# Batch 1's query and key loads in six-row pieces with 128x128 transposes, and the last output rows in two column halves

## The chip, the cores and the metric

The kernel runs on one core of a Trainium2 chip. The metric is the device time of one execution in microseconds. The kernel before took 255.05 us, the median of six runs (254.12 to 255.78).

## The reference

Attention over 4 batches of 8 heads, 768 positions and 64 dimensions per head, with a mask that keeps the first 4 positions (the sinks) and a window of 128; then a gated feed-forward layer over the 3072 tokens (512 wide, 1536 hidden).

```python
scores = scale * np.matmul(q, k.transpose(0, 1, 3, 2))
keep = is_sink | in_window
scores = np.where(keep, scores, -1000000000.0)
a = np.exp(scores - np.max(scores, axis=-1, keepdims=True))
attn_out = np.matmul(a / (np.sum(a, axis=-1, keepdims=True) + 1e-09), v)
x = attn_out.transpose(0, 2, 1, 3).reshape(B * S, H * D)
gate = np.maximum(x @ w_gate, 0.0)
out = gate * (x @ w_val) @ w_out
```

## The kernel before

Two heads make a unit; unit i belongs to batch i // 4. A unit's queries and keys are needed with the dimension on the partitions (64 of each head), in bf16. They get there in three ways:

- Batch 0, in halves (`load_half`, `cast_half`, `T_half`), with transposes on TensorE.
- Batch 1 (units 4 to 7): `load_kq` (L111) loads with (head, position group of 12) on the partitions, so that each partition holds 12 consecutive rows of one head; `cast_kq` (L145) makes bf16 on GpSimd; `T` (L275) turns the tile on TensorE in 64x64 pieces (L282), 12 for each of the two heads and each of key and query. ScalarE copies the turned keys out of PSUM (L286), VectorE the queries (L287), and VectorE then lays out the odd key tiles (L199) and the sinks (L195) beside the keys.
- Batches 2 and 3 (units 8 to 15): `load_rows` (L173) loads six rows of both heads to a partition, `cast_rows` (L178) casts on GpSimd, `to_dram` (L183) writes the result to DRAM (query first, then key), and `turn` (L188) reads it back by a DMA with transpose. GpSimd lays out the odd tiles and the sinks.

Scores are made in segments (`Sg`, L314): matmuls into a pair of PSUM banks (L324), exponential on ScalarE (L328), mask on VectorE (L335). The two pairs of banks alternate for all callers of `pair()`, so a segment waits until the pair's last reader is done; the queries turned by `T` lie in such a pair too, the keys in bank G[3]. `W` (L382) multiplies the exponentials by the values, and VectorE divides by the sum (L393, L394).

The order of work is written out by hand: 96 slots, each with one chunk of the feed-forward layer (`chunk`, L410: gate matmuls L417, Relu on ScalarE L420, value matmuls L422, product on VectorE L424). A table `plan` gives the attention steps that follow a chunk, and a table `prep` the loads and casts ahead of it. `T` of units 4 to 7 follows the chunks of slots 11, 12, 15 and 16; their scores run in slots 13 to 20. Unit 8's scores begin in slot 25 and unit 9's in slot 27. Each engine works through its instructions in this order, and so do the queues that issue DMAs: SP issues nearly all of them, GpSimd those of the weights.

The second layer (`ffn2`, L431) multiplies 128 tokens' hidden values by the output weights in 12 matmuls of 512 columns (L437); ScalarE copies the bank to SBUF (L441) and SP stores it (L442). These matmuls fill in behind the chunks; the last six tiles of 128 tokens follow, partly or wholly, the last chunk, with three banks in turn.

Of the kernel before, what the change touches and what calls it, by code (L numbers as in the profile page):

```python
# [9 lines left out]
F32 = mybir.dt.float32  # L10
BF16 = mybir.dt.bfloat16
# [8 lines left out]
def kernel(  # L20
# [12 lines left out]
    nc = tc.nc  # L33
    B, H, S, D = q.shape
# [3 lines left out]
    d_model, d_ff = moe_w_gate.shape  # L38
    KO = d_model // 128
    FM = d_ff // 128  # L40

    NR, PR = 12, 64

    const = ctx.enter_context(tc.tile_pool(name="const", bufs=1))
    gspool = ctx.enter_context(tc.tile_pool(name="gsp", bufs=3))
    outpool = ctx.enter_context(tc.tile_pool(name="outp", bufs=3))
# [3 lines left out]
    NQ, NE, NT = 3, 4, 4  # L50
    kf = [const.tile([128, S], F32, name=f"kf{i}") for i in range(NQ)]
    qf = [const.tile([128, S], F32, name=f"qf{i}") for i in range(NQ)]
# [4 lines left out]
    qT = [x[:, 0:S] for x in KQ]  # L57
# [4 lines left out]
    qn = [const.tile([128, S], BF16, name=f"qn{i}") for i in range(2)]  # L62
    kn = [const.tile([128, S], BF16, name=f"kn{i}") for i in range(2)]
    wg = const.tile([128, KO, d_ff], BF16, name="wg")
    wv = const.tile([128, KO, d_ff], BF16, name="wv")
    wo = const.tile([128, FM, d_model], BF16, name="wo")
    xT = [const.tile([128, NP, S], BF16, name=f"xT{i}") for i in range(2)]
    hT = [const.tile([128, FM, S], BF16, name=f"hT{i}") for i in range(2)]
    ident = const.tile([128, 128], BF16, name="ident")
# [38 lines left out]

    U = [Unit(i) for i in range(B * NP)]

    def load_kq(u):  # L111
        for x, dst in ((k, kf[u.i % NQ]), (q, qf[u.i % NQ])):
            nc.sync.dma_start(out=dst[:], in_=x[u.b, 2 * u.p:2 * u.p + 2].rearrange("h (p n) d -> (h p) (n d)", n=NR))


    HALF = S // 2
    half = lambda bufs, c: bufs[c // 2 % len(bufs)][:, c % 2 * HALF:c % 2 * HALF + HALF]
# [24 lines left out]
    def cast_v(b, j, rows=128, copy=nc.gpsimd.tensor_copy):  # L142
        copy(vn[b % 2][0:rows, j, :, 0:64], vf[0:rows, j, :, :])  # L143

    def cast_kq(u):  # L145
        for src, dst in ((kf[u.i % NQ], kn[u.i % 2]), (qf[u.i % NQ], qn[u.i % 2])):
            nc.gpsimd.tensor_copy(dst[:], src[:])

    def gate(u):

        nc.scalar.copy(kf[u.i % NQ][0:1, 0:2], warm[0:1, :])
# [2 lines left out]
    ND = 2 * NP  # L154
# [14 lines left out]
        for x in range(2):  # L169
            ready[u.b, u.p, x] = True  # L170


    def load_rows(u):  # L173
        for x, dst in ((q, qf), (k, kf)):
            nc.sync.dma_start(out=dst[u.i % NQ][:].rearrange("p (h e) -> p h e", h=2),
                              in_=x[u.b, 2 * u.p:2 * u.p + 2].rearrange("h (p n) d -> p h (n d)", n=6))

    def cast_rows(u):  # L178
        for src, dst in ((qf, qn), (kf, kn)):
            nc.gpsimd.tensor_copy(dst[u.i % 2][:].rearrange("p (n h d) -> p h n d", n=6, h=2),  # L180
                                  src[u.i % NQ][:].rearrange("p (h n d) -> p h n d", n=6, h=2))

    def to_dram(u):  # L183
        for i, x in enumerate((qn, kn)):
            nc.sync.dma_start(out=kqd[u.i - ND][i * S:i * S + S, :].rearrange("(p n) c -> p (n c)", n=6),
                              in_=x[u.i % 2][:])

    def turn(u):  # L188
# [86 lines left out]
    def T(u):  # L275
        t = u.i % NT
        tk, tq = G[3][:], pair()[:, 0, :]
        for x, ps in ((kn[u.i % 2], tk), (qn[u.i % 2], tq)):
            for n in range(NR):
                for h in range(2):  # L280
                    r = slice(64 * h, 64 * h + 64)
                    nc.tensor.transpose(ps.bitcast(BF16)[r, 64 * n:64 * n + 64], x[r, 64 * n:64 * n + 64], ident[r, r])  # L282
        vk, vq = (ps.bitcast(BF16)[:, 0:S].rearrange("d (n p) -> d p n", p=PR) for ps in (tk, tq))
        e = kE[t]
        to = lambda ap: ap.rearrange("d (p n) -> d p n", n=NR)
        nc.scalar.copy(to(e[:, 0:S]), vk)  # L286
        nc.vector.tensor_copy(to(qT[t]), vq)  # L287
        odd_tiles(u, nc.vector.tensor_copy)

    def T_half(c):  # L290
# [140 lines left out]
    def ffn2(b, t, m):  # L431
        if m == 0:
            ops = OP[tail[0]]
            opn[0] += 1
            opend[b, t] = ops[opn[0] % len(ops)]
        op = opend[b, t]
        nc.tensor.matmul(out=op, lhsT=hT[b % 2][:, m, t * 128:(t + 1) * 128], rhs=wo[:, m, :],  # L437
                         start=m == 0, stop=m == FM - 1)
        if m == FM - 1:
            ot = outpool.tile([128, d_model], F32, name="ot")  # L440
            nc.scalar.copy(ot[:], op)  # L441
            nc.sync.dma_start(out=out[b * S + t * 128:b * S + (t + 1) * 128, :], in_=ot[:])  # L442

    with tc.manual_schedule():
# [112 lines left out]
        for s, (b, g, m) in enumerate(slots):  # L557
            for x in prep[s]:
                if x[0] == "kq":
                    cast_kq(U[x[1]])  # L560
                elif x[0] == "load":
                    if x[1] < 7:
                        gate(U[x[1]])
                    load_kq(U[x[1]])
                elif x[0] == "half":
                    cast_half(x[1])
                elif x[0] == "w":
                    load_w(*x[1:])
                elif x[0] == "wo":
                    for c in range(3):  # L570
                        load_wo(c)
                elif x[0] == "rows":
                    load_rows(U[x[1]])
                elif x[0] == "castrows":
                    cast_rows(U[x[1]])
                elif x[0] == "td":
                    to_dram(U[x[1]])
                elif x[0] == "setup3":
                    setup3()
                elif x[0] == "setup2":  # L580
                    setup2(x[1])
                elif x[0] == "xd":
                    x_to_dram(U[x[1]])
                elif x[0] == "xturn":
                    x_turn(U[x[1]])
                elif x[0] == "turn":
                    turn(U[x[1]])
                elif x[0] == "sinks":
                    odd_tiles(U[x[1]], nc.gpsimd.tensor_copy)
                elif x[0] == "lv":  # L590
                    for j in x[2:] or range(7):
                        load_v(x[1], j)
                else:
                    cast_v(*x[1:])
            chunk(b, g, m)
            if s == 23:
                f2 += [lambda t=t, mm=mm: ffn2(0, t, mm) for t in range(6) for mm in range(FM)]
            for what, i, x in plan[s]:
                if what == "F":
                    for _ in range(i):  # L600
                        f2.popleft()()
                elif what == "X":
                    X(U[i])
                elif what == "T":
                    T(U[i])
                elif what == "H":
                    T_half(NP + i)
                elif what == "S":
                    Sg(U[i], x)
                elif what == "W":  # L610
                    W(U[i])
                else:
                    V(U[i], x)
            for _ in range(3 if s > 23 else 0):
                if f2:
                    f2.popleft()()
            if b > 0 and m == FM - 1:
                f2 += [lambda b=b, t=t, mm=mm: ffn2(b, t, mm) for t in range(3 * g, 3 * g + 3) for mm in range(FM)]
# [38 lines left out]
```

The softmax here doesn't subtract the row's maximum and nothing guards it: scores larger than these inputs give would overflow.

## Time and profile before

| what | value |
|---|---|
| the profiled execution | 254.73 us, its span 253.0 us |
| TensorE busy | 239.3 us (95% of the span) |
| VectorE busy | 131.0 us |
| ScalarE busy | 117.3 us |
| GpSimd busy | 68.1 us |
| query copies of units 4 to 7 on VectorE (L287) | 4 of 0.944 us |
| key copies of units 4 to 7 on ScalarE (L286) | 4 of 0.80 us |
| granted TensorE clock, mean | 0.997 |
| moved by DMA | 40.09 MB, mean 158 GB/s |

Time in the profile is counted from the start of the span. A line of the timeline gives start, length, engine, line of the kernel, operation, tiles and shapes, and how many instructions were merged; in brackets stands the engine's idle time just ahead of it and what ended it. The chain that ended last is followed back from the last instruction: at each step to what released it, or to the instruction before it on its engine. PE is TensorE, DVE VectorE, ACT ScalarE, POOL GpSimd, SP the engine that issues DMAs.

### The profile page before, as it was taken

How to read it: one execution, taken by the hardware profiler on the slowest of the kernel's cores; microseconds unless marked ns; L12 is line 12 of the kernel's file. 1: busy time of each engine (PE TensorE's matmuls, PEld its weight loads, DVE VectorE, ACT ScalarE, POOL GpSimd, SP SyncE). 2: the span in 40 equal slices, each digit the busy share in tenths (PEclk: the TensorE clock that was granted, in tenths of full speed). 3: DMA queues.
4: the chain of work that ended last, by engine and by line, in shares of the span. 5: the costliest groups of instructions: out<-in, count | busy, mean ns of one | idle time of the engine just before them, and what ended most of it. 6: DMA issues, size and time to landing. Idle time of an engine off the chain costs nothing.

```text
span 253.0 us, 5586 instructions
## 1 busy us (share of the span) xinstructions
PE 239.3 (95%) x2197; PEld 140.4 (55%) x2219; DVE 131.0 (52%) x249; ACT 117.3 (46%) x215; POOL 68.1 (27%) x118
## 2 busy tenths in 40 slices
PE   7779999898999799999999999999999999999993
PEld 2445566566675456666555556666555555555441
DVE  7586889999892556654225465744223222322000
ACT  3656942585854654542345674532333332333111
POOL 6694494777024227403003700000000000000000
PEclk9999999999999999999999999999999999999998
DMA  7999999999999999979899711433211101111132
GB/s 188 276 258 192 192 179 340 279 237 259 268 248 234 191 225 318 299 212 213 169 189 240 142 41 33 114 98 75 79 44 43 41 0 44 43 41 44 48 118 83
DMA packets 75571, 40.09 MB, mean 158 GB/s; under 512 B 53529, under 2 KB 71449, under 8 KB 75545
## 3 DMA queue, kind: packets, MB, share of 16 engines
q1 hardware_dynamic: 67080, 34.62, 54.6%
q0 software_dynamic: 7920, 4.72, 13.1%
q8 instruction: 17, 0.28, 0.5%
q10 hardware_dynamic: 544, 0.39, 0.5%
q14 instruction: 10, 0.07, 0.1%
HBM read 28.48 MB, written 11.25 MB: 157 GB/s over the span
## 4 chain that ended last, share of the span: by engine, by line
PE 83%; DVE 8%; ACT 5%; issue 2%; POOL 0%; DVEq 0%; ACTq 0%
PE g L417 23%; PE g L422 23%; PE g L437 21%; PE pp L324 5%; PE pp L388 4%; ACT ee L328 3%; PE pp L437 3%; PE pp L343 1%; DVE KQ L287 1%; DVE ee L335 1%; DVE hT L424 1%; PE g L343 1%; ACT ot L441 1%; DVE KQ L309 1%; DVE KQ L225 1%
## 5 line engine op out<-in xcount | busy, mean ns | idle before, releaser
L424 DVE TENSOR_TENSOR hT<-gs,g 128x384 bf16<-128x384 f32 x96 | 53.0, 552 | 81.0 <-PE g L422 79.8
L420 ACT ACTIVATE gs<-g 128x384 f32<-128x384 f32 x96 | 47.6, 495 | 81.8 <-PE g L417 79.0
L417 PE MATMUL g<-xT,wg 128*128 128x384 bf16 x384 | 78.3, 326 | 0.2 <-DVE xT L367 0.2
L422 PE MATMUL g<-xT,wv 128*128 128x384 bf16 x384 | 78.1, 326 | 0.0
L437 PE MATMUL g<-wo,hT 128*128 128x512 bf16 x231 | 62.8, 379 | 2.0 <-issue 1.0
L417 PEld LDWEIGHTS <-wg 128*128 128x128 bf16 x384 | 36.0, 98 | 31.5 <-issue 0.5
L328 ACT ACTIVATE ee<-pp 128x998 bf16<-128x998 f32 (+4 forms) x52 | 44.8, 906 | 15.5 <-PE pp L324 15.4
L422 PEld LDWEIGHTS <-wv 128*128 128x128 bf16 x384 | 37.6, 98 | 24.8
L437 PEld LDWEIGHTS <-hT 128*128 128x128 bf16 x288 | 26.6, 98 | 25.1 <-issue 0.7
L335 DVE TENSOR_TENSOR ee<-ee,msk 128x838 bf16<-128x838 bf16 (+3 forms) x44 | 30.3, 698 | 12.8 <-ACT ee L328 12.3
L143 POOL CAST vn<-vf 128x512 bf16<-128x512 f32 x28 | 18.5, 666 | 46.6 <-DMA vf<-in_v_dram 46.5
L441 ACT COPY ot<-g 128x512 f32<-128x512 f32 x21 | 12.3, 587 | 19.0 <-PE g L437 19.0
L324 PE MATMUL pp<-KQ 64*128 64x252 bf16 (+7 forms) x320 | 16.8, 223 | 3.7 <-DVE KQ L287 1.3
L324 PEld LDWEIGHTS <-KQ 64*128 64x128 bf16 x320 | 10.8, 94 | 13.2 <-issue 8.5
L388 PEld LDWEIGHTS <-ee 128*128 128x128 bf16 x384 | 13.2, 97 | 1.6
L388 PE MATMUL pp<-vn,ee 128*128 128x65 bf16 x384 | 13.5, 193 | 0.0
L394 DVE TENSOR_TENSOR xn<-pp,rn 128x896 bf16<-128x896 f32 x12 | 13.1, 1092 | 0.4
L180 POOL CAST qn<-qf 128x768 bf16<-128x768 f32 x8 | 7.6, 955 | 20.0 <-DMA kqd<-qn 15.2
L437 PE MATMUL pp<-wo,hT 128*128 128x512 bf16 x36 | 8.1, 379 | 0.0
L180 POOL CAST kn<-kf 128x768 bf16<-128x768 f32 x8 | 7.0, 871 | 2.4 <-DMA kf<-in_k_dram 1.9
L273 PE MATMUL g<-idle 128*128 128x512 bf16 x14 | 5.3, 517 | 1.3 <-DVE warm L212 1.3
L308 ACT COPY KQ<-g 128x384 bf16<-128x384 bf16 (+3 forms) x15 | 3.9, 349 | 2.4 <-PE g L301 2.2
(90 smaller groups left out, 135.5 us busy)
## 6 DMA issues: line engine op xcount, KB each, us to landing
out_dram<-ot SPq DMA_DIRECT2D x24, 256.0 KB
kf<-in_k_dram SPq DMA_DIRECT2D x12, 384.0 KB
qf<-in_q_dram SPq DMA_DIRECT2D x12, 384.0 KB
vf<-in_v_dram SPq DMA_DIRECT2D x12, 256.0 KB
vf<-in_v_dram SPq DMA_DIRECT2D x12, 224.0 KB
kf<-in_k_dram SPq DMA_DIRECT2D x8, 192.0 KB
wg<-in_moe_w_gate_dram POOLq DMA_DIRECT2D x6, 256.0 KB, 7.7
wv<-in_moe_w_val_dram POOLq DMA_DIRECT2D x6, 256.0 KB, 8.9
```

The lines of the kernel that those rows point to most:

```text
L143: copy(vn[b % 2][0:rows, j, :, 0:64], vf[0:rows, j, :, :])
L180: nc.gpsimd.tensor_copy(dst[u.i % 2][:].rearrange("p (n h d) -> p h n d", n=6, h=2), src[u.i % NQ][:].rearrange("p (h n d) -> p h n d", n= ...
L324: nc.tensor.matmul(out=ps[:, h, c0:c1], lhsT=kE[t][64 * h:64 * h + 64, x0:x0 + 128], rhs=qT[t][64 * h:64 * h + 64, q0:q0 + c1 - c0], start ...
L328: nc.scalar.activation(x, ps[:, :, b0:n], Act.Exp, bias=0.0, scale=scale)
L335: nc.vector.tensor_tensor(x, x, m.unsqueeze(1).to_broadcast([128, 2, c1 - c0]), op=Alu.mult)
L388: nc.tensor.matmul(out=ps[:, h, 65 * t:65 * t + 65], lhsT=ee[u.i % NE][:, g, h, c0:c0 + 128], rhs=vn[u.b % 2][:, j, 2 * u.p + h, 0:65], st ...
L417: nc.tensor.matmul(out=gp[:, 0:CUT], lhsT=wg[:, ko, m * 128:(m + 1) * 128], rhs=x[:, ko, c], start=ko == 0, stop=ko == KO - 1)
L420: nc.scalar.activation(gs[:], gp[:, 0:CUT], Act.Relu, bias=0.0, scale=1.0)
L422: nc.tensor.matmul(out=vp[:, 0:CUT], lhsT=wv[:, ko, m * 128:(m + 1) * 128], rhs=x[:, ko, c], start=ko == 0, stop=ko == KO - 1)
L424: nc.vector.tensor_tensor(h[:, m, c], gs[:], vp[:, 0:CUT], op=Alu.mult)
L437: nc.tensor.matmul(out=op, lhsT=hT[b % 2][:, m, t * 128:(t + 1) * 128], rhs=wo[:, m, :], start=m == 0, stop=m == FM - 1)
L441: nc.scalar.copy(ot[:], op)
```

## The change

1. Units 4 to 7 are loaded by `load_rows` and cast by `cast_rows`; `load_kq` and `cast_kq` are gone. Both functions now take the key first and the query second, for batches 2 and 3 as well. `to_dram` keeps its order, query first.
2. `T` turns a unit in six pieces of 128x128 for the keys and six for the queries.
3. `T` copies the queries out of PSUM on ScalarE.
4. The last 128 output rows are made in two halves of 256 columns, each with its own bank and its own 12 matmuls. The first half is copied by ScalarE and stored from SP, the second is copied by VectorE and stored from ScalarE's queue.

```diff
-    NR, PR = 12, 64
+    NR = 6
-    def load_kq(u):
-        for x, dst in ((k, kf[u.i % NQ]), (q, qf[u.i % NQ])):
-            nc.sync.dma_start(out=dst[:], in_=x[u.b, 2 * u.p:2 * u.p + 2].rearrange("h (p n) d -> (h p) (n d)", n=NR))
-    def cast_kq(u):
-        for src, dst in ((kf[u.i % NQ], kn[u.i % 2]), (qf[u.i % NQ], qn[u.i % 2])):
-            nc.gpsimd.tensor_copy(dst[:], src[:])
     def load_rows(u):
-        for x, dst in ((q, qf), (k, kf)):
+        for x, dst in ((k, kf), (q, qf)):
             nc.sync.dma_start(out=dst[u.i % NQ][:].rearrange("p (h e) -> p h e", h=2),
-                              in_=x[u.b, 2 * u.p:2 * u.p + 2].rearrange("h (p n) d -> p h (n d)", n=6))
+                              in_=x[u.b, 2 * u.p:2 * u.p + 2].rearrange("h (p n) d -> p h (n d)", n=NR))
     def cast_rows(u):
-        for src, dst in ((qf, qn), (kf, kn)):
+        for src, dst in ((kf, kn), (qf, qn)):
...
         for x, ps in ((kn[u.i % 2], tk), (qn[u.i % 2], tq)):
             for n in range(NR):
-                for h in range(2):
-                    r = slice(64 * h, 64 * h + 64)
-                    nc.tensor.transpose(ps.bitcast(BF16)[r, 64 * n:64 * n + 64], x[r, 64 * n:64 * n + 64], ident[r, r])
+                c = slice(128 * n, 128 * n + 128)
+                nc.tensor.transpose(ps.bitcast(BF16)[:, c], x[:, c], ident[:])
...
         nc.scalar.copy(to(e[:, 0:S]), vk)
-        nc.vector.tensor_copy(to(qT[t]), vq)
+        nc.scalar.copy(to(qT[t]), vq)
         odd_tiles(u, nc.vector.tensor_copy)
...
+        if b == B - 1 and t == 5:
+            if m == 0:
+                for x, bank in enumerate((op, OP[1][opn[0] % 3 - 1])):
+                    c = slice(d_model // 2 * x, d_model // 2 * x + d_model // 2)
+                    for i in range(FM):
+                        nc.tensor.matmul(out=bank[:, 0:d_model // 2], lhsT=hT[b % 2][:, i, t * 128:(t + 1) * 128],
+                                         rhs=wo[:, i, c], start=i == 0, stop=i == FM - 1)
+                    ot = outpool.tile([128, d_model], F32, name="ot")
+                    (nc.scalar.copy, nc.vector.tensor_copy)[x](ot[:, c], bank[:, 0:d_model // 2])
+                    (nc.sync, nc.scalar)[x].dma_start(out=out[b * S + t * 128:b * S + (t + 1) * 128, c], in_=ot[:, c])
+            return
...
-                    cast_kq(U[x[1]])
+                    cast_rows(U[x[1]])
...
-                    load_kq(U[x[1]])
+                    load_rows(U[x[1]])
```

## The prediction, made before the result was known

> **What bounds the kernel now.** I read the chain that ended last, then TensorE's idle gaps, then, at each gap, the queue that released it.
>
> ```profile
> PE 83%; DVE 8%; ACT 5%; issue 2%; POOL 0%; DVEq 0%; ACTq 0%
> ```
>
> TensorE is the bound overall, so a change pays where TensorE waits, or ahead of its first or behind its last matmul. TensorE's timeline from 20 us on has four waits of 0.29 us or more (time, length, instruction, and in brackets the idle time before it and who ended it):
>
> ```profile
> 50.20 0.40 PE L324 MATMUL pp<-KQ 64*128 64x252 bf16 x6 [1.03 <-DVE KQ L287]
> 60.41 0.39 PE L324 MATMUL pp<-KQ 64*128 64x244 bf16 x6 [0.29 <-DVE KQ L287]
> 62.94 0.62 PE L324 MATMUL pp<-KQ 64*128 64x252 bf16 x14 [0.73 <-DVE xn L394]
> 86.75 0.28 PE L324 MATMUL pp<-KQ 64*128 64x252 bf16 x4 [0.92 <-POOL KQ L195]
> ```
>
> The first three, 2.05 us, lie in batch 1's score stage, where VectorE is full (9.34 of 10.00 us from 43.5, 9.41 of 9.44 us after it) and the query copy L287 is among what is late. The fourth is the entry to batch 2. GpSimd's timeline shows why it is late:
>
> ```profile
> 78.12 0.50 POOL L199 COPY KQ<-KQ 128x372 bf16<-128x372 bf16 x1 [0.59 <-DMA KQ<-kqd]
> 78.56 0.19 POOL L195 COPY KQ<-KQ 128x12 bf16<-128x12 bf16 x1
> ...
> 85.50 0.61 POOL L143 CAST vn<-vf 128x512 bf16<-128x512 f32 x1 [5.73 <-DMA vf<-in_v_dram]
> 86.06 0.50 POOL L199 COPY KQ<-KQ 128x372 bf16<-128x372 bf16 x1
> 86.50 0.19 POOL L195 COPY KQ<-KQ 128x12 bf16<-128x12 bf16 x1
> ```
>
> Unit 9's odd-tile copy stands on GpSimd behind a value cast that waits 5.73 us for a DMA. That DMA was issued on SP at 80.21 behind transposes issued at 70.58 and 75.07; the first of these waited for unit 8's write to DRAM (issued 60.20, landed 70.44). From 38 to 74 us the 16 DMA engines show a busy share of about 1. So a queue of transfers sets when batch 2 may start, and none of it waits for TensorE after 54 us. Unit 8 is ready at 78.75 and TensorE comes at 80.41: 1.66 us of slack. Unit 9 has none.
>
> The end of the kernel, in the timeline:
>
> ```profile
> 246.39 2.75 PE L437 MATMUL g<-wo,hT 128*128 128x512 bf16 x12
> 249.22 0.58 ACT L441 COPY ot<-g 128x512 f32<-128x512 f32 x1 [2.00 <-PE g L437]
> ```
>
> The store is issued at 249.83, its first packet moves at 250.67, its last ends at 251.46, the span ends at 253.02.
>
> **The change, part by part.**
>
> *Transposes.* Per unit 24+24 of 64x64 become 6+6 of 128x128. The chain in order of time (start, length):
>
> ```profile
> 44.24 0.49 PE g L282 x24
> 44.73 0.38 PE pp L282 x24
> 45.11 0.76 PE g L417 x4
> ...
> 70.97 0.39 PE g L402 x7
> 71.36 0.65 PE g L417 x4
> ```
>
> L402 is the new form: 0.39/7 = 56 ns each, so 12 x 56 = 0.67 us for 0.87; and the gate matmuls behind a 128-row operation take 0.65, not 0.76. Saved: 0.31 for three units, some 0.15 for the one followed by scores: 1.08 us. A rule speaks against it: the Trainium skill, "TensorE: Matmul & The Clock Gate", Part 4 (PE-mode transpose), gives about 275 ns for such a transpose inside a kernel. By it 48 would take 13.2 us against 3.5 now, a loss of 9.7; by the row 2.7. The row is this very instruction, back to back; I take it.
>
> *Query copies.* VectorE loses 4 x 0.944 = 3.8 us; ScalarE gains 4 x 0.80 (L286, same shape) = 3.2 us. New wait: the gate Relu, and exponentials, queue behind them. By ScalarE's rows each slot of this stage then holds 2.4 to 3.1 us of its work. Walking the stage with these rows: unit 4's query copy ends at 46.1, unit 5's at 48.1, the two first scores follow at 48.2 and 48.6 with no wait, the next group starts near 49.0 instead of 50.53. Later ScalarE and the batch-1 value casts (GpSimd ends them at 57.70) limit it. The two waits on L287 go, part of the third stays: TensorE is 1.5 to 2.5 us early at 64 us. Bounds: 3.1 (all waits and 1.08), and 0 if ScalarE becomes full.
>
> *Where that goes.* From 64 us TensorE runs unhindered to batch 2, where the transfers have not moved: unit 8 not before 78.75, unit 9 not before 86.69. What is late next is therefore the 86.75 wait itself, which grows by what was saved. I book **0**. If that cover were gone, the 1.5 to 2.5 would count.
>
> *Loads of units 4 to 7.* The same eight issues on SP (0.33 to 0.42 us each; the six-row form 0.37 to 0.53, no path), but 256 pieces of 1536 bytes, not 128 of 3072. The windows (last two columns: DMA share, GB/s) with old form and, in batch 3's loads, new form:
>
> ```profile
> 44.00:45.00 1.00, 1.00 (x50) 0.83 (x48) 0.97 (x3) 0.34 (x2) 0.84 (x2) 1.00 1.02 409
> 45.00:46.00 1.00, 1.00 (x14) 0.60 (x7) 1.00 (x5) 0.67 (x2) 0.88 (x2) 1.00 1.04 412
> ...
> 100.00:101.00 1.00, 1.00 (x7) 0.59 (x6) 0.96 (x1) 0.12 (x1) 1.00 (x4) 1.00 1.07 401
> 101.00:102.00 1.00, 1.00 (x18) 0.55 (x17) 0.40 (x1) 0.49 (x2) 0.79 (x2) 1.00 1.06 398
> ```
>
> By GB/s: 3.15 MB at 411 or 400 is 7.65 or 7.86 us, +0.2. By the trace's single packets (median 121 ns for 3072 bytes, 65 for 1536): 64 x 121 = 7.74 or 128 x 65 = 8.32 us on each engine, +0.58. By successive landings: 1.007 us per load (43.31 to 46.33, three steps) or 1.06 (99.55 to 102.73), x 8 = +0.43. The skill's rule ("DMA: Bandwidth & Descriptors", Specifications) is that pieces of 512 bytes or more go at line rate: +0. I take the rows, **+0.45** (0.2 to 0.6). The engines are full behind these loads, so the delay reaches unit 8's write, its transpose, and unit 9's value cast.
>
> *Casts.* Same count; GpSimd took 0.827 us in the flat form and 0.82 to 0.83 undisturbed in the six-row form: 0. In batches 2 and 3 the key cast now goes first, but the query write is still first on SP, so unit 8's writes go out near 60.7 and 61.1 instead of 59.06 and 60.20, with unit 9's writes and unit 11's loads behind them. Cover: earlier loads (three of 384 KB) were landing until 67.9, so the writes would queue anyway: 0. With no backlog it is 0.9 to 1.6.
>
> *Last rows.* 24 matmuls of 256 columns for 12 of 512: measured steps are 56 ns at 128 columns, 162 at 384, 216 at 512, so 109 at 256: 2.62 for 2.59, +0.03. The first half's copy and store lie under the second half's matmuls. Last copy: VectorE's PSUM copies took 0.55 (384 elements) and 0.94 (768), so 0.41 at 256 for ScalarE's 0.585: -0.17. Store: the 2048-byte packets took about 85 ns, 8 an engine; 1024 bytes, on the line through the packet times above, 46: 0.37 for 0.70, -0.33. The issue moves to ScalarE's queue, used only at the start, where its first packet came 0.4 us later after the issue than SP's: +0 to +0.4; I take 0.1. Sum **-0.4** (-0.6 to 0).
>
> **Sum.** +0.45 - 0.4 = +0.05 us on the profiled execution: 254.73 (span 253.02) becomes 254.8. It lies 0.3 below the median of six, 255.05; on that the change gives 255.1.
>
> **Rivals.**
> 1. *The saving passes* (27%). The DMA behind the 86.75 wait landed on its engines between 82.80 and 85.36; another interleaving could bring its last landing to the first. Then unit 8's readiness (79.2) is what is left: at most 1.2 us earlier there, and up to 0.9 of the 86.75 wait gone. With the end's 0.4: 1.2 to 2.5 us, 252.6 to 253.9, middle 253.4. For: VectorE's relief is real. Against: everything ahead of that DMA in its queue.
> 2. *The chain to batch 2 lengthens* (23%), slower. SP issues in order, and unit 8's key write now stands behind the query write, which waits for the second cast. It decides once the backlog ahead of it is under about 1.5 us. Price 0.9 to 1.6 on top of the 0.45, less 0.4: 256.0 to 256.7, middle 256.3. Against: that backlog was some 6 us.
> 3. *ScalarE becomes full in the score stage* and the 1.5 to 2.5 us are never saved: 255.1 all the same, since batch 2's entry hides up to 0.92 + 0.45 of lateness; it belongs to the forecast.
>
> **Numbers.** Forecast 50%, its own range 254.4 to 255.8 (+0.6 to -0.6 of the two terms and the spread of the six runs, 254.12 to 255.78). A measurement can tell about 0.3%, 0.77 us, from no change. The forecast puts 0.06 below that, 0.40 within, 0.04 above; rival 1 0.25 below and 0.02 within; rival 2 0.23 above. Faster 0.31, same 0.42, slower 0.27. The range leaves out about a tenth at each side: 253.2 to 256.5.
>
> **What would show it.** Right: no wait on a query copy, 128x128 transposes in 0.34 us for six, TensorE 1.5 to 2.5 us early at 64 us; unit 8's transpose issued near 71.0; waits on POOL KQ L195 (renumbered) of together 2 to 3.5 us near 78 and 87; last matmul to end of span 3.5 us instead of 3.9. Wrong: the wait near 87 no longer than 0.9, or the transpose issued a microsecond off.

## The result, and the profile after

The changed kernel took 255.32 us, the median of 37 runs (253.27 to 258.25); the kernel before, in the same comparison, 254.21 us (74 runs, 253.06 to 256.49). The ratio is 1.0029, 95% interval 1.0013 to 1.0045: slower by about 0.7 us. A ratio leaves out a kernel's runs that lie more than 1.5% above its fastest, so I give counts and means of all runs beside it: the means of all runs are 255.44 and 254.32, 1.1 us apart.

The forecast of 255.1 held as a number, but by luck: it added 0.05 us to a median of six runs, 255.05. The kernel before took 254.21 in 74 runs, and the change came to +0.7 us by the ratio, +1.1 by the means; the base was too high by about as much as the change was too low. The place where the forecast said the saving would go was nearly right. What it did not foresee is that the wait there can also cost TensorE its clock.

The profiled execution of the changed kernel took 257.67 us (span 255.8, mean granted clock 0.991); the one of before took 254.73 (span 253.0, clock 0.997). So this profile is of one of the longer executions, and I say below which share of the runs it stands for. The page's chain by engine, and the row of the granted clock in 40 slices:

```profile
PEclk9999999999999997999999999999999999999999
...
PE 76%; ACT 6%; DMA 6%; DVE 5%; issue 4%; SPq 1%; POOL 1%; POOLq 0%; DVEq 0%; ACTq 0%
```

TensorE's share of the chain fell from 83% to 76%, and DMA, which had none, has 6%. Slice 16 (96 to 102 us) shows a reduced clock, where the row of the kernel before has none. To see when time was won and lost, I set the two traces side by side at VectorE's product, one for each of the 96 chunks (L424 before, L414 after), and took the difference in start:

| chunk (its start before, us) | after minus before, us |
|---|---|
| 9 (39.13) | +0.11 |
| 17 (61.07) | -0.72 |
| 23 (75.60) | -0.89 |
| 28 (89.19) | -1.13 |
| 30 (94.10) | -1.13 |
| 33 (101.60) | +3.29 |
| 40, 60, 95 | +3.29, +3.28, +3.29 |

Everything happens before chunk 33: 1.13 us won, then 4.42 us lost between chunks 30 and 33, and from there to the end the two run in step. The last rows give back 0.5, which makes the 2.8 us between the spans.

TensorE's timeline at the loss:

```profile
85.62 0.28 PE L314 MATMUL pp<-KQ 64*128 64x252 bf16 x4 [0.53 <-POOL KQ L186]
...
94.63 0.28 PE L314 MATMUL pp<-KQ 64*128 64x244 bf16 x2
97.66 0.72 PE L314 MATMUL pp<-KQ 64*128 64x252 bf16 x10 [2.75 <-POOL KQ L186]
98.71 1.06 PE L439 MATMUL g<-wo,hT 128*128 128x512 bf16 x2 [0.33 <-issue]
99.56 1.49 PE L407 MATMUL g<-xT,wg 128*128 128x384 bf16 x4
```

The wait at unit 9's entry, 0.92 us before (at 86.75), is 0.53 here. Unit 10's entry, where the kernel before passed with no wait (its twelve score matmuls ran as one group at 95.76), now holds TensorE for 2.75 us, released by the sinks' copy on GpSimd. And the next four gate matmuls take 1.49 us instead of 0.81. GpSimd shows what the copy stood behind:

```profile
84.37 0.61 POOL L139 CAST vn<-vf 128x512 bf16<-128x512 f32 x1 [3.61 <-DMA vf<-in_v_dram]
84.93 0.50 POOL L190 COPY KQ<-KQ 128x372 bf16<-128x372 bf16 x1
...
96.41 0.61 POOL L139 CAST vn<-vf 128x512 bf16<-128x512 f32 x1 [2.99 <-DMA vf<-in_v_dram]
96.97 0.50 POOL L190 COPY KQ<-KQ 128x372 bf16<-128x372 bf16 x1
97.41 0.19 POOL L186 COPY KQ<-KQ 128x12 bf16<-128x12 bf16 x1
```

It is the pattern of the prediction one unit later: the value cast waits 2.99 us for its DMA, and unit 10's odd tiles and sinks queue behind it. In the kernel before, this queue was done just as TensorE came:

```profile
94.75 0.61 POOL L143 CAST vn<-vf 128x512 bf16<-128x512 f32 x1 [2.62 <-DMA vf<-in_v_dram]
...
95.75 0.19 POOL L195 COPY KQ<-KQ 128x12 bf16<-128x12 bf16 x1
```

```profile
95.76 0.77 PE L324 MATMUL pp<-KQ 64*128 64x244 bf16 x12
```

So the 2.75 us have two parts. TensorE came to this group of matmuls at 94.63 instead of 95.76, 1.13 us earlier: that is the saving. And the value cast began 1.66 us later, at 96.41 instead of 94.75. The windows show the clock (third column from the end), then the DMA share and GB/s:

```profile
97.00:98.00 1.00, 0.34 (x8) 0.29 (x10) 0.00 (x0) 0.00 (x1) 0.60 (x3) 0.93 0.69 179
98.00:99.00 1.00, 0.67 (x7) 0.39 (x5) 0.00 (x0) 1.00 (x2) 0.30 (x1) 0.50 0.95 324
99.00:100.00 1.00, 1.00 (x4) 0.42 (x3) 0.86 (x2) 0.91 (x2) 0.57 (x2) 0.50 1.06 391
100.00:101.00 1.00, 1.00 (x5) 0.49 (x4) 1.00 (x1) 0.00 (x0) 0.86 (x2) 0.50 1.06 400
101.00:102.00 1.00, 1.00 (x15) 0.64 (x13) 0.13 (x2) 0.49 (x1) 1.00 (x2) 0.86 1.06 398
```

The trace's clock record has one stretch of 3.41 us at half clock, which gives the five rows' reduced values; at half clock it loses 3.41 / 2 = 1.7 us of work. With the wait, 2.75 + 1.7 = 4.45: the 4.42 us of the table.

How often it happens can be read without a trace, since every run states its mean granted clock. One such stretch in about 255 us makes 1 - 1.7 / 255 = 0.993. The runs fall into two groups with nothing between them: 0.993 and less, or 0.996 and more. Of the changed kernel's 37 runs 12 are in the lower group (mean 256.8 us; the other 25: 254.8). Of the 194 runs of the kernel before that were taken beside the experiments, 16 are (256.3; the others 254.5).

The end of the kernel:

```profile
250.99 1.47 PE L433 MATMUL pp<-wo,hT 128*128 128x256 bf16 x12
251.23 0.37 ACT L436 COPY ot<-g 128x256 f32<-128x256 f32 x1 [0.72 <-PE g L433]
252.55 0.42 DVE L436 COPY ot<-pp 128x256 f32<-128x256 f32 x1 [14.35 <-DMA out_dram<-ot]
253.01 0.37 ACTq L437 DMA_DIRECT2D out_dram<-ot  x1
```

From the start of the last copy to the end of the span it was 253.02 - 249.22 = 3.80 us before, and is 255.84 - 252.55 = 3.29 now. The first half's copy and store lie under the second half's matmuls, as intended.

### The profile page after: what moved, and what is told of

It reads as the page before. It is cut to its first block, busy times and chain, and to the rows that moved or that the text cites. A ratio compares the mean times of both kernels' runs of the same rounds, so it can differ in the third digit from the quotient of the medians.

```text
span 255.8 us, 5326 instructions
## 1 busy us (share of the span) xinstructions
PE 240.1 (94%) x2065; PEld 141.7 (55%) x2087; DVE 128.4 (50%) x246; ACT 119.3 (47%) x219; POOL 68.4 (27%) x118
## 4 chain that ended last, share of the span: by engine, by line
PE 76%; ACT 6%; DMA 6%; DVE 5%; issue 4%; SPq 1%; POOL 1%; POOLq 0%; DVEq 0%; ACTq 0%
PE g L407 22%; PE g L412 21%; PE g L439 18%; PE pp L378 4%; PE pp L314 4%; ACT ee L318 4%; PE pp L439 3%; DMA vf<-in_v_dram 3%; DMA KQ<-kqd 2%; PE pp L333 1%; PE g L333 1%; DMA out_dram<-ot 1%; DVE KQ L299 1%; DVE KQ L216 1%; ACT KQ L298 1%
## 5 line engine op out<-in xcount | busy, mean ns | idle before, releaser
L414 DVE TENSOR_TENSOR hT<-gs,g 128x384 bf16<-128x384 f32 x96 | 53.0, 552 | 82.8 <-PE g L412 81.1
L439 PE MATMUL g<-wo,hT 128*128 128x512 bf16 x219 | 60.5, 382 | 2.2 <-issue 1.1
L439 PEld LDWEIGHTS <-hT 128*128 128x128 bf16 x276 | 25.5, 98 | 24.0 <-issue 1.2
L139 POOL CAST vn<-vf 128x512 bf16<-128x512 f32 x28 | 19.0, 689 | 43.6 <-DMA vf<-in_v_dram 43.6
L443 ACT COPY ot<-g 128x512 f32<-128x512 f32 x20 | 11.7, 587 | 17.0 <-PE g L439 17.0
L171 POOL CAST kn<-kf 128x768 bf16<-128x768 f32 x12 | 10.0, 832 | 26.4 <-DMA kqd<-kn 16.7
L171 POOL CAST qn<-qf 128x768 bf16<-128x768 f32 x12 | 10.2, 847 | 3.8 <-PE pp L378 1.6
```

The lines of the kernel that those rows point to most:

```text
L414: nc.vector.tensor_tensor(h[:, m, c], gs[:], vp[:, 0:CUT], op=Alu.mult)
```

## The experiments

Each was measured beside the kernel before. The table gathers them; the lower clock means 0.993 and less, and brackets hold what the kernel before had beside it.

| kernel | ratio, 95% interval | runs | with the lower clock | mean of the other runs, us |
|---|---|---|---|---|
| after | 1.0029 (1.0013 to 1.0045) | 37 | 12 | 254.8 |
| tail_only | 0.9996 (0.9966 to 1.0026) | 14 | 3 (9 of 59) | 254.0 (254.3) |
| split_loads | 1.0015 (0.9989 to 1.0041) | 14 | 0 (9 of 59) | 254.6 (254.3) |
| query_first | 0.9994 (0.9970 to 1.0018) | 22 | 8 (9 of 59) | 254.2 (254.3) |
| query_copy | 0.9964 (0.9941 to 0.9987) | 22 | 1 (9 of 59) | 253.6 (254.3) |
| long_loads | 1.0002 (0.9969 to 1.0036) | 14 | 7 (0 of 51) | 254.0 (254.7) |
| row_loads | 0.9998 (0.9981 to 1.0016) | 22 | 0 (0 of 51) | 254.6 (254.7) |
| copy_tail | 0.9965 (0.9944 to 0.9986) | 22 | 3 (0 of 51) | 253.6 (254.7) |
| late_casts | 1.0176 (1.0135 to 1.0217) | 6 | 6 (0 of 51) | none |
| after_odd_dve | 0.9978 (0.9950 to 1.0006) | 22 | 9 (3 of 57) | 253.7 (254.5) |
| before_odd_dve | 0.9994 (0.9973 to 1.0016) | 22 | 1 (3 of 57) | 254.4 (254.5) |
| copy_tail_odd_dve | 0.9936 (0.9914 to 0.9958) | 20 | 2 (3 of 57) | 252.9 (254.5) |
| waits_off | 0.9953 (0.9929 to 0.9977) | 22 | 4 (4 of 27) | 253.0 (254.5) |

**The parts alone.** Four kernels take one part each: the last rows, the size of the loads' pieces, the order of query and key, and the query copies.

*tail_only* is the kernel before with the last rows in two halves:

```diff
+        if b == B - 1 and t == 5:
+            if m == 0:
+                for x, bank in enumerate((op, OP[1][opn[0] % 3 - 1])):
...
+                    (nc.scalar.copy, nc.vector.tensor_copy)[x](ot[:, c], bank[:, 0:d_model // 2])
...
```

> The kernel before with the last 128 rows in two column halves and nothing else. In the profile of the changed kernel the time from the last PSUM copy's start to the end of the span is 3.25 us, against 3.80 before. My theory: the halves gain 0.5 us of 254.2, ratio 0.998, and the changed kernel's loss lies wholly in batch 1 and 2. Rival: the halves' gain is eaten by something ahead of the end, ratio 1.000.

Measured 253.97 us against 254.37, ratio 0.9996. In its profile, last copy to end of span took 252.0 - 248.71 = 3.3 us, as in the changed kernel. The gain of half a microsecond is visible in two traces; the times alone, with an interval of 0.6%, neither confirm nor exclude it.

*split_loads* is the kernel before with each load of units 4 to 7 cut into pieces of 1536 bytes (data as before, the tiles padded so that the pieces don't merge):

```diff
-    kf = [const.tile([128, S], F32, name=f"kf{i}") for i in range(NQ)]
+    kf = [const.tile([128, 2, 392], F32, name=f"kf{i}") for i in range(NQ)]
...
-            nc.sync.dma_start(out=dst[:], in_=x[u.b, 2 * u.p:2 * u.p + 2].rearrange("h (p n) d -> (h p) (n d)", n=NR))
+            nc.sync.dma_start(out=dst[:, :, 0:384], in_=x[u.b, 2 * u.p:2 * u.p + 2].rearrange("h (p a n) d -> (h p) a (n d)", a=2, n=NR // 2))
...
```

> The kernel before, but units 4 to 7 are loaded in pieces of 1536 bytes and not 3072 (the staging tiles get a gap of 8 elements between the two halves of a row), in the same layout, transposes and copies as before. My theory: the smaller pieces alone hold the transfers ahead of batch 2 back, by 0.45 us as predicted, and 1.0 to 1.5 us by the last engines' landings in the changed kernel's profile; TensorE waits that much longer at 86 to 98 us: ratio 1.002 to 1.006. Rival (order of the casts and writes is what holds batch 2 back): ratio 1.000.

Measured 254.45 against 254.37, means of all runs 0.03 us apart. The last of these loads landed at 48.81 us, a microsecond later than in the kernel before (47.84), but unit 8's transpose was issued at 70.80 (70.58 before). The delay was there and did not travel.

*query_first* is the changed kernel with the old order, query ahead of key, in batches 2 and 3:

```diff
-        for x, dst in ((k, kf), (q, qf)):
+        for x, dst in ((k, kf), (q, qf)) if u.i < ND else ((q, qf), (k, kf)):
...
-        for src, dst in ((kf, kn), (qf, qn)):
+        for src, dst in ((kf, kn), (qf, qn)) if u.i < ND else ((qf, qn), (kf, kn)):
```

> The changed kernel with one part undone: in batches 2 and 3 the query is loaded and cast first again, as before. My theory: the order costs nothing, because the writes queue behind earlier loads anyway: same as the changed kernel, ratio to before 1.003. Rival (the order is the cause): unit 9's query write goes out at 61 and not at 66 us, unit 11's loads at 64 and not at 68, batch 2 is not held back, and the changed kernel's loss of 0.7 us turns into the gain of the last rows: ratio 0.998.

Measured 254.80 against 254.37; means of all runs 0.78 us apart, 8 of 22 runs with the lower clock. Its profile has the same wait and the same half clock as the changed kernel's:

```profile
97.45 0.85 PE L314 MATMUL pp<-KQ 64*128 64x252 bf16 x10 [2.69 <-POOL KQ L186]
```

Unit 9's query write moved from 66.17 to 61.66 us, as it should have. Unit 8's transpose was still issued only at 72.10, against 72.77 in the changed kernel. So the order moved the write and not what followed from it, and the wait is there without the new order.

*query_copy* is the kernel before with the query copies on ScalarE:

```diff
-        nc.vector.tensor_copy(to(qT[t]), vq)
+        nc.scalar.copy(to(qT[t]), vq)
```

> The kernel before, but the query copies of units 4 to 7 on ScalarE. My theory: the waits of TensorE at 50 and 60 us (1.3 us in all) go, TensorE is 1 to 1.5 us earlier at 64 us, and the wait near 87 us grows by as much: ratio 1.000. Rival (the score stage's time reaches the end): ratio 0.995.

Measured 253.59 against 254.37, ratio 0.9964 (0.9941 to 0.9987): 0.9 us faster, and the interval excludes no change. The saving that I had booked at nothing arrives. One profile shows how it can arrive, on GpSimd at unit 9's and unit 10's entries:

```profile
83.26 0.61 POOL L143 CAST vn<-vf 128x512 bf16<-128x512 f32 x1 [3.88 <-DMA vf<-in_v_dram]
83.81 0.50 POOL L199 COPY KQ<-KQ 128x372 bf16<-128x372 bf16 x1
...
93.06 0.61 POOL L143 CAST vn<-vf 128x512 bf16<-128x512 f32 x1 [2.33 <-DMA vf<-in_v_dram]
93.62 0.50 POOL L199 COPY KQ<-KQ 128x372 bf16<-128x372 bf16 x1
```

The value tile came at 83.2 us, not at 85.4 as in the profile of before, and TensorE entered unit 9 without a wait; unit 10's tile came at 93.0, and TensorE waited 0.51 us there. At chunk 40 this execution is 1.70 us ahead of the profiled one of before.

**Is it the form of the loads?** In the changed kernel's profile the transfers ahead of batch 2 run about 2 us later (unit 8's transpose at 72.77 instead of 70.58), and the order did not explain it, so my next theory was the six-row loads. Two kernels exchange the form of the loads of units 4 to 7 alone; in both, batch 1's rows then reach wrong places, so that part of the output is not the reference's.

*long_loads*, the changed kernel with the old form:

```diff
+            if u.i < ND:
+                nc.sync.dma_start(out=dst[u.i % NQ][:],
+                                  in_=x[u.b, 2 * u.p:2 * u.p + 2].rearrange("h (p n) d -> (h p) (n d)", n=12))
+                continue
```

> The changed kernel, but the loads of units 4 to 7 move 3072 bytes a piece again, in the layout of before, while casts, 128x128 transposes and copies stay as changed: batch 1's queries and keys are thus wrong data, the amount of work is the same, and only its time is read. My theory now: the form of these eight loads is what costs, since it makes the slowest DMA engine 1.6 us later at their end and everything queued behind them late; with the long pieces the savings of transposes, query copy and last rows all reach the end: about 252.3 us, ratio 0.992. Rival (something else in the changed part, TensorE's or ScalarE's other timing, holds the transfers back): ratio 1.000 to 1.003, with unit 8's transpose still issued at 72 us.

*row_loads*, the kernel before with the new form:

```diff
-            nc.sync.dma_start(out=dst[:], in_=x[u.b, 2 * u.p:2 * u.p + 2].rearrange("h (p n) d -> (h p) (n d)", n=NR))
+            nc.sync.dma_start(out=dst[:].rearrange("p (h e) -> p h e", h=2), in_=x[u.b, 2 * u.p:2 * u.p + 2].rearrange("h (p n) d -> p h (n d)", n=6))
```

> The kernel before, but units 4 to 7 are loaded as in the changed kernel (six rows of both heads to a partition); transposes and copies stay, so batch 1's queries and keys are wrong data and only the time is read. My theory: the loads' last landing comes 1.6 us later (49.5 instead of 47.8), the loads of unit 8 go out at 53.9 and not 52.7, unit 8's transpose at 72 and not 70.6, and batch 2 starts later: ratio 1.004 to 1.007. If it is only the size of the pieces, it equals the split loads, 1.0015, with unit 8's transpose at 70.8. Rival (the loads are harmless by themselves): 1.000.

long_loads took 255.44 against 254.61 (means of all runs 0.83 us apart, 7 of 14 runs with the lower clock), row_loads 254.63 against 254.61 (0.12 us less in the mean, none of 22). The theory fell: the old form in the new kernel does not remove the loss from the mean (the 7 runs with full clock do lie 0.7 us below those of before), and the new form in the old kernel does not bring it. In long_loads' profile the loads had ended by 48.02, and still unit 8's transpose came at 73.52 and TensorE waited:

```profile
97.10 0.84 PE L318 MATMUL pp<-KQ 64*128 64x252 bf16 x10 [2.92 <-POOL KQ L190]
```

In row_loads' profile TensorE was held for 1.56 us at unit 9's entry (87.54), with no loss of clock.

**Where the wait comes from, and what it costs.** *copy_tail* takes the two parts that touch no load: the query copies on ScalarE and the last rows in halves, on the kernel before (diffs as in query_copy and tail_only).

> The kernel before with two parts of the change: query copies on ScalarE and the last rows in two halves; loads, casts and transposes as before. Both savings are there and the loads are not slowed: 0.9 us from the copy and 0.4 to 0.55 from the last rows, 253.0 us, ratio 0.9945. If the two savings hide each other: ratio 0.997.

Measured 253.82 against 254.61, ratio 0.9965 (0.9944 to 0.9986). Its own profile, however, is one of the 3 of its 22 runs with the lower clock, at 256.85 us, and shows the mechanism at unit 9's entry:

```profile
87.81 0.28 PE L324 MATMUL pp<-KQ 64*128 64x252 bf16 x4 [2.04 <-POOL KQ L195]
88.02 0.82 PE L449 MATMUL g<-wo,hT 128*128 128x512 bf16 x3
88.68 0.97 PE L417 MATMUL g<-xT,wg 128*128 128x384 bf16 x4
89.45 1.48 PE L422 MATMUL g<-xT,wv 128*128 128x384 bf16 x4
90.73 1.48 PE L449 MATMUL g<-wo,hT 128*128 128x512 bf16 x3
```

After a wait of 2.04 us the first matmuls still run at full speed. About 1.4 us later a group of three takes 1.48 us where the same took 0.82, so the clock can fall well after the wait that provokes it, and the matmuls that look slow are not the ones that were late. (The last section shows what sets the delay.) This kernel has the old loads, the old order and the old transposes, and still its unit 8's transpose was issued at 73.13.

*late_casts* was meant to take the cover away from unit 10's odd tiles: the changed kernel with batch 2's value casts one slot later.

```diff
-                prep[s1 + j].append(("v", b, j))
+                prep[s1 + j + (b == 2)].append(("v", b, j))
```

> The changed kernel with batch 2's value casts one slot later in the order of GpSimd, so that the odd-tile copies of units 9 and 10 no longer stand behind a value cast that waits for a DMA landing at 84 and 96 us. My theory: TensorE's waits on these copies (0.5 and 2.75 us in the changed kernel's profile) vanish or shrink below 0.5 us, and what the score stage saved reaches the end: 252.5 to 253.3, ratio 0.993 to 0.996. Rival: unit 10's keys or the values themselves are late and take the place of that wait: ratio 1.000 to 1.003.

A miss: 259.19 against 254.61, ratio 1.0176 (1.0135 to 1.0217). The last value cast now stood behind a cast of unit 12, which waits for its own load, and TensorE waited for the values:

```profile
101.18 1.15 PE L378 MATMUL pp<-vn,ee 128*128 128x65 bf16 x18 [4.62 <-POOL vn L139]
102.14 1.47 PE L439 MATMUL g<-wo,hT 128*128 128x512 bf16 x3
```

It says nothing on unit 10, but it prices the clock: with a wait of 4.62 us came 6.83 us at half clock, twice 3.41, and all six runs have the lower clock (0.986 in four, 0.992 and 0.993 in two).

*after_odd_dve* takes the wait away in another manner. VectorE, not GpSimd, makes the odd tiles and sinks of units 9 to 11, so that they stand behind no value cast:

```diff
-                    odd_tiles(U[x[1]], nc.gpsimd.tensor_copy)
+                    odd_tiles(U[x[1]], nc.vector.tensor_copy if 9 <= x[1] <= 11 else nc.gpsimd.tensor_copy)
```

> The changed kernel with the odd-tile and sink copies of units 9 to 11 on VectorE, ahead of the same chunks, so that they no longer stand on GpSimd behind batch 2's value casts. My theory: what the change saves is lost in TensorE's wait for unit 10's odd tiles (2.75 us in the profile) and in the 3.41 us at half clock that follow it; without that wait both go, and what is late next is unit 8's second part, the values' last cast near 99 us (a wait of about 1.5 us, too short for the clock). About 252.3 us, ratio 0.991 to 0.994, no row at half clock before the end. Rival (the transfers hold batch 2 back in any order, or VectorE's waits stall the chunks): ratio 1.000 to 1.003.

*before_odd_dve* is the same line in the kernel before.

> The kernel before with the same move of the odd-tile copies of units 9 to 11 to VectorE. It loses the 0.9 us wait at 86.75 and little else, because it comes later to unit 10: ratio 0.996 to 0.998. By my theory the changed kernel with the same move is 1.0 to 1.8 us faster than this one, since nothing hides the score stage's saving and the last rows' any more; by the rival the two stand as before and after do, 0.7 us apart the other way.

*copy_tail_odd_dve* is the same line in copy_tail.

> Query copies on ScalarE, last rows in two halves, odd tiles of units 9 to 11 on VectorE; loads, casts, order and 64x64 transposes of batch 1 as before. A version that may beat both. By my theory it lacks only the transposes' 1.1 us, of which batch 2's values hide a part, and has the shorter transfers: 252.0 to 252.8, ratio 0.990 to 0.994. If the loads and the order of the changed kernel cost something of their own, it is faster than the changed kernel with the same move; if not, slower by up to 1 us.

In the kernel before the line does nothing (0.9994, means of all runs 0.06 us apart): its wait at unit 9, 0.92 us in the one profile, does not show in the times. In the changed kernel the waits on odd tiles at unit 10 are gone, and the time comes to 254.58 against 254.36, 0.9978 (0.9950 to 1.0006); but 9 of 22 runs still have the lower clock, and the mean of all runs is 0.34 us above before's. Its profile, of a run with clock 0.998, shows what is late next, on TensorE and on GpSimd:

```profile
99.25 0.70 PE L378 MATMUL pp<-vn,ee 128*128 128x65 bf16 x18 [1.96 <-POOL vn L139]
```

```profile
98.58 0.61 POOL L139 CAST vn<-vf 128x512 bf16<-128x512 f32 x1 [1.72 <-DMA vf<-in_v_dram]
```

The last value tile itself landed at 98.53: it was issued on SP at 94.18, behind unit 11's transpose. In copy_tail_odd_dve, whose profile is one of its 2 runs with the lower clock, the same wait, also of 1.96 us, did halve the clock for 3.41 us:

```profile
98.62 0.70 PE L388 MATMUL pp<-vn,ee 128*128 128x65 bf16 x18 [1.96 <-POOL vn L143]
```

The median of copy_tail_odd_dve is the best of all kernels here: 252.99 against 254.36, 0.9936 (0.9914 to 0.9958).

*waits_off* takes both waits from the changed kernel: VectorE's odd tiles as above, and batch 2's last value loads issued ahead of unit 11's transpose.

```diff
-                prep[s0 + j].append(("lv", b, j))
+                prep[min(s0 + j, 24) if b == 2 else s0 + j].append(("lv", b, j))
```

> The changed kernel with the odd-tile copies of units 9 to 11 on VectorE and, besides, batch 2's last value loads (tiles 4 to 6) issued on SP ahead of unit 11's transpose instead of behind it. The remaining wait, 1.96 us on the values' last cast at 99.25 (in the changed kernel with the odd-tile move alone), should go: that tile would land near 95 and not at 98.5. My theory: with both covers gone the change's savings reach the end, and no run is long enough idle for half clock: 251.0 to 252.5, ratio 0.987 to 0.993, no run above 256 us (11 of 37 of the changed kernel are). Rival (the changed part itself makes the slow runs, whatever waits follow it): runs above 256 us remain about one in three, ratio 0.997 or more.

Measured 253.21 against 254.79, ratio 0.9953 (0.9929 to 0.9977): with the two waits gone the changed kernel beats the one before by 1.2 us in the ratio. Its 4 of 22 runs with the lower clock are no larger a share than the 4 of 27 of the kernel before beside it. That speaks for the loss lying in these waits and in what followed them. Two limits: the earlier value loads were not tried in the kernel before, so that some of the 1.2 us may be theirs alone; and the gain is less than the 251.0 to 252.5 that I had expected even in the runs with full clock (253.0). TensorE's waits in its profile, whose mean clock is 1.000 and whose span is 250.6 us (waited for: us in total, times, longest):

```profile
PE g L264 <- DVE warm L203: 1.3, 1, 1.3
PE pp L378 <- POOL vn L139: 1.2, 3, 0.5
PE g L439 <- issue: 1.0, 6, 0.2
```

No wait for L186 is left among them, and the three for L139 are those of batch 1's values, near 59 us.

## Why the prediction was right or wrong

*Transposes: right.* Six and six stand in the trace as the row of L402 had it, in 0.67 us together, and the gate matmuls behind them step in 0.65:

```profile
44.19 0.50 PE L272 MATMUL g<-ident,kn 128*128 128x128 bf16 x6
44.52 0.50 PE L272 MATMUL pp<-ident,qn 128*128 128x128 bf16 x6
44.86 0.81 PE L407 MATMUL g<-xT,wg 128*128 128x384 bf16 x4
45.51 0.81 PE L412 MATMUL g<-xT,wv 128*128 128x384 bf16 x4
```

From start to start it is 0.33 us for six, 55 ns each; the second number of a line also holds the time to the modelled end. The 275 ns of the rule in the prediction (the Trainium skill, "TensorE: Matmul & The Clock Gate", Part 4, PE-mode transpose), taken as the step from each to the next, would have been wrong by a factor of five.

*Query copies: right in kind, too high in size for this execution.* The first scores followed at 48.22 (forecast 48.2) and no wait on a query copy is left. TensorE was 1.71 us early at chunk 13 but only 0.72 at chunk 17, not 1.5 to 2.5. The rest went to what the walk named, the value casts and the division, and to one thing that it had not:

```profile
58.33 0.22 PE L378 MATMUL pp<-vn,ee 128*128 128x65 bf16 x2 [0.30 <-POOL vn L139]
58.88 0.70 PE L378 MATMUL pp<-vn,ee 128*128 128x65 bf16 x18 [0.33 <-POOL vn L139]
...
62.23 0.62 PE L314 MATMUL pp<-KQ 64*128 64x252 bf16 x14 [0.92 <-DVE xn L384]
```

VectorE's odd-tile copy and sinks of unit 7 took 1.84 and 1.49 us (57.18 to 60.4) where the same two had taken 0.29 and 0.15 for unit 5, and the division came late. In other executions of kernels with the same copies the lead at this point was 0.7 (waits_off), 1.0 (query_first), 1.1 (copy_tail), 1.2 (query_copy), 1.5 (after_odd_dve and copy_tail_odd_dve), 2.3 (long_loads) and 2.8 us (late_casts), so this profile is below the forecast's range and the others lie on both sides of it. Counted from chunk 9, the gain was 0.8 us where VectorE's two copies of unit 7 took 3.3 us together (the changed kernel), 1.4 where they took 2.5 (waits_off, query_first), and 2.2 and 2.9 where they took 1.1 (copy_tail, late_casts); the last section shows what stretches them. Some of the lead is plain scatter: before_odd_dve, which changes nothing ahead of this point, was 1.4 us later here than the profile of before.

*"Where that goes: I book 0": the failing step.* The saving did run into batch 2's entry in this profile, but neither where nor at what price I had put it. First, the place: in the changed kernel unit 9's value tile landed about 84.3, a microsecond sooner than in the profile of before, and TensorE passed with 0.53 us; the queue caught up at unit 10. Second, the cover is not a fixed wall: query_copy gains 0.9 us, and over the 14 traces the cast of this tile began anywhere from 82.45 to 86.20, so the 85.50 of the one trace of before was on the late side. I had given that, as rival 1, 27%. Third, and not foreseen by any case: a wait is not a neutral place for a saving to vanish. TensorE that comes earlier waits longer, and from about 2 us of wait the clock may halve for 3.41 us. The absorbed 1.1 us alone would have made a wait of about that length, which cost no clock in any trace here. With unit 10's value tile 1.66 us later as well it became 2.75, and cost 1.7 more. Why the tile was later is open (below).

How much of the measured loss is this? The changed kernel's runs with the lower clock are 2.05 us longer than its others and 12 of 37: 0.66 us of the mean. The kernel before has 16 of 194 at 1.8 us: 0.15. So the clock makes about 0.5 of the 1.1 us between the means of all runs, if before had the same share in the comparison with the changed kernel, where its clocks are not on record. The other 0.6 is also in runs with full clock (254.8, where those of before had 254.5 beside the experiments).

*Loads: the size was right at the source, the step to the end was wrong.* In the windows where the old form had moved 409 and 412 GB/s, the new one moved these (last column):

```profile
44.00:45.00 1.00, 1.00 (x16) 0.87 (x14) 0.95 (x2) 0.51 (x2) 0.80 (x2) 1.00 1.05 392
45.00:46.00 1.00, 1.00 (x9) 0.59 (x7) 1.00 (x5) 1.00 (x2) 0.77 (x2) 1.00 1.07 396
```

3.15 MB at 394 is 8.0 us for 7.65, +0.35, within the 0.2 to 0.6. But the delay was to reach unit 9's value cast and did not: with the new form alone, row_loads' and split_loads' means of all runs are -0.12 and +0.03 us from the kernel before. The +0.45 of the sum should have been near 0, with the sum then at -0.4.

*Casts and their order (rival 2): not shown.* The write moved as that rival said. But its price, 0.9 to 1.6 us at batch 2's entry, didn't come back when query_first undid it.

*Last rows: right.* 0.5 us in the trace for a forecast of 0.4 (0 to 0.6). The copies took 0.37 (ScalarE) and 0.42 (VectorE) for 0.41.

*What I had named as signs.* Unit 8's transpose was to be issued near 71.0, and a microsecond off would be wrong: it was 72.77. By my own sign the transfers' chain was not understood. The wait near 87 was to grow beyond 0.9 us, and it was 0.53; the long one stood at 97.66, where I had named none.

*What stays open.* First, why that chain ran about 2 us later in the changed kernel's profile: order and form of the loads, undone one at a time, left the transpose at 72.1 and 73.5. The changed loads are not needed for it: copy_tail and copy_tail_odd_dve, which lack them, had it at 73.13 and 73.45, and before_odd_dve, where nothing ahead of it is changed, at 71.98. On the chip that ran tail_only, split_loads and query_copy it came between 70.70 and 70.87, and at 72.10 in query_first; on the two other chips it never came before 71.69. So scatter between executions, or the chip, may be as much of a cause as the change; which chip ran the profiled kernel before is not on record, and nothing here separates the two. Second, the 0.6 us in runs with full clock (0.3 by the means 254.8 and 254.5). Against the -0.4 of the mended sum that is 0.7 to 1.0 us with no cause shown. The table hints that both parts matter there: undoing the order or the form leaves means of 254.2 and 254.0 for 254.8, but these rest on 14 and 7 runs that spread over more than 2 us and were not taken beside the changed kernel, and the intervals of the ratios touch. The 128x128 transposes without any other part of the change weren't tried. Third, the changed kernel's runs with lower clock have no trace but one; that their wait is the same one is argued from the count in waits_off (4 of 22) against 12 of 37, 8 of 22 and 7 of 14, not seen. Why copy_tail_odd_dve, with fewer parts of the change, does as well as waits_off isn't settled either.

## What to carry to other kernels

A saving that you expect a later wait to absorb makes that wait longer. Work out how long it becomes, and from about 2 us on charge half of 3.41 us for TensorE's clock, in a share of the runs. Before you call a transfer's landing a wall, ask how far it moves from run to run; here the same tile came up to 3.7 us later in one trace than in another. And if you make TensorE earlier, move the copies that gate its next stage off the queue in which they stand behind a late transfer at the same time: with that, two parts of this change gave 0.64% (copy_tail_odd_dve) instead of 0.35% without it (copy_tail; the intervals overlap), where the whole change without it cost 0.29%.

## What the runs showed of the hardware that was not expected

*TensorE's clock falls after waits much shorter than the time for which it stays low.* In these profiles stretches at half clock came with single waits of 2.04, 2.69, 2.75, 2.92 and 4.62 us, and with one of two waits of 1.96 us; none came with a wait of 1.73 us or less. They lasted 3.41 us, or twice that. The Trainium skill, "TensorE: Matmul & The Clock Gate", Part 1 (HAM oscillation), warns of idle gaps above about 3.4 us, and says that the clock is judged over windows of that length which run freely. The length agrees, but as a limit for a gap 3.4 us is too generous by these runs.

The traces show the windows. In all 14 every stretch of the clock's record, between one change and the next, is a whole number of 3.413 us: the 92.16 us at full clock ahead of the changed kernel's fall are 27, copy_tail's 81.92 are 24. The first change comes anywhere from 3.98 to 7.28 us, so the windows do not start with the kernel. Laid out from each record's own changes, they say how much of a wait falls into one of them:

| kernel | wait, us (its end) | of it in one window, us | clock in the next window |
|---|---|---|---|
| late_casts | 4.62 (101.18) | 3.40, then 1.23 | half, half |
| after | 2.75 (97.66) | 2.75 | half |
| long_loads | 2.92 (97.10) | 2.64, then 0.28 | half, full |
| query_first | 2.69 (97.45) | 2.14, then 0.55 | half, full |
| copy_tail | 2.04 (87.81) | 2.02 | half |
| copy_tail_odd_dve | 1.96 (98.62) | 1.96 | half |
| after_odd_dve | 1.96 (99.25) | 0.87, then 1.09 | full, full |
| row_loads | 1.73 (63.32) | 1.48, then 0.25 | full, full |

So about 2 us of idle TensorE inside one window halved the clock for the next, and the same wait of 1.96 us cost nothing where a border cut it in two. Every fall at a kernel's end fits: it follows the first window with 2.09 us or more behind the last matmul, and query_first's clock stayed up after a window with 1.96. Only late_casts' second half-clock window followed less idle time, 1.23 us, and there the clock was already low. The borders also set the delay. In query_first's windows the clock was half already in the microsecond in which the wait ended, in copy_tail's only some 1.4 us after it. The border lay at 96.90 in the one, inside the wait, and at 89.20 in the other:

```profile
97.00:98.00 1.00, 0.55 (x8) 0.44 (x10) 0.00 (x0) 0.10 (x1) 0.95 (x3) 0.50 1.08 267
98.00:99.00 1.00, 1.00 (x8) 0.30 (x5) 0.07 (x1) 1.00 (x2) 0.66 (x1) 0.50 0.92 296
```

*A small copy on VectorE can take six times its usual time.* Unit 7's odd tiles in the changed kernel took 1.84 us from 57.18, its sinks 1.49 us from 58.95 (first fence), and on GpSimd there stood, with hardly a gap (second fence):

```profile
57.18 1.84 DVE L190 COPY KQ<-KQ 128x372 bf16<-128x372 bf16 x1
58.95 1.49 DVE L186 COPY KQ<-KQ 128x12 bf16<-128x12 bf16 x1
```

```profile
57.09 1.74 POOL L139 CAST vn<-vf 128x512 bf16<-128x512 f32 x3
58.76 0.89 POOL L171 CAST kn<-kf 128x768 bf16<-128x768 f32 x1
59.60 0.82 POOL L171 CAST qn<-qf 128x768 bf16<-128x768 f32 x1
```

The first copy ends at 59.02, 0.19 us after the three value casts, the second at 60.44, as the query cast does (60.42). Unit 5's odd tiles, 0.29 us from 47.52, began just before the end of one cast (47.66) and were done before the next (47.88). The 14 traces hold many such copies of odd tiles. From 40 us on, the 17 that started while GpSimd did nothing took 0.27 to 0.29 us, even the five during which a cast then began. Those that started while a cast still had 0.29 us or more to run took 0.42 to 1.84 us and ended, save the one of 1.84, 0.13 to 0.15 us after a cast's end: the running cast's in most, the second or third in a row in four. The Trainium skill, "SBUF — State Buffer", section "SBUF: two separate sides", has VectorE and GpSimd share a pair of ports that one of them holds for a whole instruction while the other is blocked. These times fit it, though a copy can be blocked through two or three casts in a row. Moved copies fit too: of unit 10's odd tiles, which VectorE makes in four kernels, two that met a running cast took 0.69 us and two that did not 0.28.
